# A second Strassen level for a third product: 82 matmul steps per output stage become 81

## The chip, the core and the metric

The kernel runs on one core of a Trainium2 chip. The metric is the device time of one execution in microseconds (us). Three runs of the kernel before took 2226.53, 2226.63 and 2226.74 us, a median of 2226.63 us.

## The reference

A convolution over the last seven positions of a sequence, with one softmax-normalised kernel per head, feeds a two-layer block with the hardswish activation. All of it is in float32.

```python
w = softmax(weight)                      # (8 heads, 7 taps)
x_pad = zeros(6 positions) ++ x          # x: (8, 4096, 192)
y[b, s, c] = sum_k w[head(c), k] * x_pad[b, s + k, c]
y = y.reshape(32768, 192)
h = y @ w_in                             # (192 -> 2048)
g = h * clip(h + 3, 0, 6) / 6
out = g @ w_out                          # (2048 -> 192)
```

## The kernel before

**Blocks.** The 32768 tokens are worked through in 32 blocks of 1024 (`NB`). Block 0 is handled by code of its own, in which the weights are prepared too. Each of the other 31 blocks runs `first_layer` and then `second_layer`. While block i is in its second layer, the convolution result `y` of block i+1 is split into three float32 parts (`split_high`, `split_rest`), which are swapped between the partition halves by DMA into `y_other` (`swap_parts`, six DMAs of 384 KB), and the input of block i+2 is loaded (`begin_conv`). The convolution steps (L919, L921) are placed among the other work.

**First layer.** 16 units (`count`) each compute 128 of the 2048 hidden channels for one pairing of token halves, 18 matmuls per unit. ScalarE (ACT) rescales the sum in PSUM and takes the relu, VectorE (DVE) multiplies (`gate`, L306) and writes into the tile `g`. A unit occupies one of four slots of two PSUM banks. Units 0 to 7 use `y_own`, units 8 to 15 `y_other`.

**Second layer as a Strassen product.** `g` is a 2 x 2 block matrix: rows are token halves of 512, columns halves of the hidden channels, 8 chunks of 128 each, named A11, A12, A21, A22. `w_out` is split in the same way. The Winograd form takes seven products instead of eight:

```
S1 = A21 + A22    S2 = S1 - A11    S3 = A11 - A21    S4 = A12 - S2
P1 = A11 B11   P2 = A12 B21   P3 = S4 B22   P4 = A22 T4
P5 = S1 T1     P6 = S2 T2     P7 = S3 T3
```

The sums are stored in place: S1 over A21, S2 over A11, and both S3 and S4 in the tile `s3`. So S1 needs S3 to have been formed, S2 needs P1 to be done with A11, and S4 needs P7 to be done with S3. S3 is formed pair of chunks by pair of chunks at the end of the first layer (three pairs on GpSimd, POOL, the last one on DVE). S1 is formed for two pairs by an adding DMA from POOL's queue (L557) and for the other two on DVE (L559). S2 and S4 are formed on DVE (`g_sums`, L412), four chunks at a time.

**Four streams.** A product has 96 output columns, in three quarters of 32. TensorE's array is used as four strips of 32 columns; `second_layer` writes one list of matmuls per strip (`streams`, `clock`), and sorts all of it by time. One step is half a matmul of 512 tokens, or one matmul of 256. Streams 0 to 2 take one quarter each of the plain products (`plain`, 8 matmuls of two steps per quarter). Stream 3 takes P1 and P5, whose first two quarters are computed with a second Strassen level (`small`): seven products of 4 matmuls of 256 tokens, over sums made by `small_sums` (L578) and weights made by `small_weights`. Their third quarter is plain. All streams have 82 steps:

```
streams 0, 1, 2:  P4  P7 (with one chunk of P1's third quarter)  P2  P6  P3
stream 3:         P1 (second level)  P5 (second level)
```

A finished accumulator is carried on by ACT copies: from one small accumulator to the next (`steps`), or from strip to strip, since a strip of the array writes only its own 32 partitions. `do(t, ...)` puts work of the other engines at step t of the program's order. Each engine works through its own part of that order and waits where an operand isn't ready; PE does so too, so a late operand in one stream stops all four.

**Tiles and banks.** Three of the four PSUM slots hold the accumulators d, e, b, x_, a and c; the fourth is free for the next first layer, except in the last block, where P3 is computed by token halves in it (`plain_by_halves`, `end_lower`, `end_upper`). The small accumulators A, B, C, E and V lie in the fourth strip's rows of banks that the other streams use too. `y_other` lies in a pool of its own (tag "other"), `p1` beside `s3`.

Of the kernel before, what the change touches and what calls it, by code (L numbers as in the profile page):

```python
# [25 lines left out]
def kernel(  # L26
# [93 lines left out]
    w_s = cst.tile([P, 2, 4, NP // 2, QS], F32, name="w_s")  # L120
# [144 lines left out]
    def swap(to, part):  # L265
        nc.sync.dma_start(out=to[D2:P], in_=part[0:D2])
        nc.sync.dma_start(out=to[0:D2], in_=part[D2:P])
# [222 lines left out]
    def swap_parts():  # L490
        y_other[0] = pools[0].tile([P, 3, K3, N], F32, name="y_other", tag="other")
        for n in range(3):
            swap(y_other[0][:, n], y_own[n])


    def first_layer(i, jobs):
# [92 lines left out]
    def second_layer(i, between):  # L589
        last = i + 1 == NB  # L590
        ours = [free_slots.pop(0) for _ in range(3)]
        d, e, b, x_, a, c = (psum[:, 2 * n + k] for n in ours for k in range(2))
        ends = [psum[:, 2 * free_slots[0] + k] for k in range(2)] if last else [b, b]
# [35 lines left out]
        def small(n, m_, out, start=False):  # L629

            x, w = prod[n]
            sums, ws = (s1[-1], w_s[:, 0]) if n == 1 else (s5, w_s[:, 1])
            x11, x12, x21, x22 = four_parts(x)
            z1, z2, z3, z4 = four_parts(sums)
            b11, b12, b21, b22 = (
                w_out[:, h::2, w, q * QS : (q + 1) * QS] for h in range(2) for q in range(2)
            )
            t1, t2, t3, t4 = (ws[:, k] for k in range(4))
            xm, wm = {
                1: (x11, b11), 2: (x12, b21), 3: (z4, b22), 4: (x22, t4),  # L640
                5: (z1, t1), 6: (z2, t2), 7: (z3, t3),
            }[m_]
            for u in range(NP // 2):
                put(3, 1, lambda u=u: matmul(
                    3, out[:, lo], wm[:, u], xm[:, u], start and u == 0
                ))
# [9 lines left out]
        def tiles():  # L656
            new_results()
            if last:
                xts.insert(0, NP - 1)
            late.update(zip(("p7", "p5", "u3"), (results[0][m, n] for n in range(3))))  # L660

        for q in range(NQ):
            plain(q, d, 4, q, every, True)
            before = (1, 6, NP)[q]
            plain(q, c, 7, q, every[:before], True)
            plain(q, e, 1, 2, range(5 + q, 6 + q))
            do(clock[q], copy, out=e[rows(q + 1)] if q < 2 else p1[third], in_=e[rows(q)])
            plain(q, c, 7, q, every[before:])
            plain(q, a, 2, q, every[:6], True)
            plain(q, b, 6, q, every)  # L670
            plain(q, a, 2, q, every[6:])
            if last:
                plain_by_halves(q, 3, q, 0)
                plain_by_halves(q, 3, q, 1)
            else:
                plain(q, b, 3, q, every)

        def level_two(n, p, chunks, order):
# [3 lines left out]
            def fill_half(t, k):  # L682
                for _ in range(k):
                    ch = left[t].pop(0)
                    x, w = prod[n]
                    put(3, 1, lambda ch=ch: matmul(
                        3, (ends[0], x_)[t][fourth, halves[t]], w_out[:, ch, w, 2 * QS : 3 * QS],
                        x[:, ch, halves[t]], ch == 0,
                    ))

            def fill(k):
# [3 lines left out]
                1: lambda: copy(out=B[:, lo], in_=A[:, lo]),  # L695
                2: lambda: copy(out=p()[first, lo], in_=A[:, lo]),
                6: lambda: copy(out=C[:, lo], in_=B[:, lo]),
                5: lambda: copy(out=p()[second, lo], in_=E[:, lo]),
                7: lambda: add(p()[second, hi], C[:, lo], p()[second, lo]),
                3: lambda: add(p()[second, lo], B[:, lo], p()[second, lo]),  # L700
                4: lambda: copy(out=p()[first, hi], in_=C[:, lo]),
            }
            to = {1: A, 2: A, 6: B, 5: E, 7: C, 3: B, 4: C}
            for step in order.split():
# [4 lines left out]
                else:  # L709
                    k = int(step)  # L710
                    small(n, k, to[k], k in (1, 5))
                    do(clock[3], steps[k])

        level_two(1, lambda: p1, range(5), "1 x5 6 5 2 7 3 4")
        do(14, copy, out=e[first], in_=V)
# [7 lines left out]
        for t, n in ((16.2, 1), (16.2, 2), (30.5, 3), (34.5, 4)):  # L723
            do(t, small_sums, s5, S1, (n,), nc.vector)
        do(32, tiles)
        do(34, lambda: copy(out=late["p7"], in_=c[m]))
# [3 lines left out]
        do(62, lambda: add(late["u3"], b[m], late["p7"]))  # L730
# [3 lines left out]
        do(66, lambda: store(i, p1, 0, 0))  # L734
# [9 lines left out]
        def end_lower():  # L744
            p5, u3, c12 = late["p5"], late["u3"], results[0][m, 6]
            two = slice(0, 2 * QS)
            copy(out=p5[third, lo], in_=ends[0][fourth, lo])
# [10 lines left out]
        def end_upper():  # L758
            p5, u3, c12 = late["p5"], late["u3"], results[0][m, 6]
            copy(out=p5[third, hi], in_=x_[fourth, hi])  # L760
# [4 lines left out]
            add(c12[third, hi], x_[fourth, hi], c12[third, hi])  # L765
# [3 lines left out]
        if last:  # L769
            do(74, end_lower)  # L770
        else:
            do(82, lambda: copy(out=late["p5"][third], in_=V))
# [28 lines left out]
    with tc.manual_schedule():  # L801
# [125 lines left out]
        def split_y():  # L927
            high, low, mix = y_own
            high_of(high[:], y[:])
            split_rest()  # L930
# [4 lines left out]
        def split_rest():  # L935
            high, low, mix = y_own
            nc.vector.tensor_tensor(out=r32(low[:]), in0=y[:], in1=high[:], op=ALU.subtract)
            from_high(mix[:], high[:], 1.0 + EPS, y[:], ALU.subtract)
# [29 lines left out]
        p1 = last.tile([DH, N], F32, name="p1")  # L968
        left = []
        for i in range(1, NB):  # L970
# [10 lines left out]
            if i + 1 < NB:  # L981
                between = [(13, split_high), (15, split_rest), (18, swap_parts)]
# [36 lines left out]
```

## Time and profile before

| | us |
|---|---|
| median of three runs | 2226.63 |
| profiled execution, span from first to last instruction | 2224.9 |
| median of the runs less that span | 1.7 |
| first layer, start to start (988.70 to 1021.60) | 32.90 |
| second layer (953.23 to 988.70) | 35.47 |
| POOL: one small sum L578, 128x256, in a row of its kind | 0.74 |
| POOL: one subtraction L412, 128x1024, mean | 3.07 |
| ACT: copy 32x256, PSUM to PSUM / to SBUF | 0.34 / 0.37 |
| ACT: copy 32x512, PSUM to PSUM / to SBUF | 0.55 / 0.58 |

A line of a group reads: line of the kernel, engine, operation, output<-inputs, shapes, count | busy us, mean ns of one | idle time before, and what ended it. A line of a stage has the stretch from the span's start, its length, then each engine's busy time with its number of instructions, the granted clock, the DMA engines' mean busy share and GB/s. PEld is TensorE's weight load, which overlaps its matmuls. A float32 matmul appears as two instructions in the profile. A line of the timeline has start, duration, engine, line and operation.

### The profile page before, as it was taken

The numbers are of one execution on the slowest core, as the hardware profiler recorded it, in microseconds if no ns is written. First come the engines' busy times: TensorE is split into PE (matmuls) and PEld (weight loads), VectorE is DVE, ScalarE is ACT, GpSimd is POOL, SyncE is SP. The second block draws the span as 40 slices with busy tenths as digits, with TensorE's granted clock in tenths as the row PEclk, the third lists the DMA queues.
The fourth block names the chain that finished last, engine by engine and source line by source line (L and its number), as shares of the span: only waits on it lengthen the run. The fifth ranks groups of instructions, "written<-read, shape, count | busy, mean of one in ns | idle before, by whom it ended". The sixth has DMA issues, their size and how long they took to land.

```text
span 2224.9 us, 50339 instructions
## 1 busy us (share of the span) xinstructions
PE 2218.0 (100%) x21496; PEld 1532.7 (69%) x21496; DVE 1894.3 (85%) x1673; ACT 1379.2 (62%) x1678; POOL 823.8 (37%) x690
## 2 busy tenths in 40 slices
PE   9999999999999999999999999999999999999999
PEld 5467776677766777766777667776677776677766
DVE  8888888888888888888888888888888888888876
ACT  7457665576655676555766557665567655576654
POOL 2344432344422444223443234442244422344323
PEclk9999999999999999999999999999999999999999
DMA  6244224443244342344422444324434234442232
GB/s 157 57 98 85 49 58 91 85 83 62 53 82 91 77 80 47 71 91 84 85 48 58 91 87 81 67 49 82 91 79 81 47 67 91 84 84 52 55 77 34
DMA packets 253584, 166.57 MB, mean 75 GB/s; under 512 B 208017, under 2 KB 213137, under 8 KB 253361
## 3 DMA queue, kind: packets, MB, share of 16 engines
q1 hardware_dynamic: 234872, 129.46, 28.4%
q0 software_dynamic: 17248, 33.64, 8.7%
q8 instruction: 168, 2.75, 0.5%
q14 instruction: 56, 0.45, 0.1%
q10 hardware_dynamic: 1240, 0.27, 0.1%
HBM read 31.72 MB, written 25.17 MB: 26 GB/s over the span
## 4 chain that ended last, share of the span: by engine, by line
PE 99%; DVE 0%; DMA 0%; ACTq 0%; issue 0%; DVEq 0%; ACT 0%
PE psum L615 49%; PE psum L508 46%; PE psum L296 2%; PE psum L341 2%; DMA x<-in_x_dram 0%; DVE y L255 0%; DVE top L175 0%; ACTq L89 0%; PE psum L816 0%; DVE results L456 0%; DVE scale L171 0%; DVE y L251 0%; DVE scale L192 0%; DVEq L1014 0%; DVE results L462 0%
## 5 line engine op out<-in xcount | busy, mean ns | idle before, releaser
L615 PE MATMUL psum<-g,w_out 128*32 128x512 f32 (+1 forms) x6712 | 967.5, 552 | 0.0
L306 DVE SCALAR_TENSOR_TENSOR g<-g,psum 128x1024 f32<-128x1024 f32 (+1 forms) x528 | 618.3, 1186 | 198.8 <-ACT g L302 194.5
L578 POOL TENSOR_TENSOR s<-g 128x256 f32<-128x256 f32 x248 | 273.6, 1103 | 1241.1 <-DVE g L306 1200.5
L302 ACT ACTIVATE g<-psum,half 128x1024 f32<-128x1024 f32 (+1 forms) x528 | 564.8, 1087 | 6.0 <-PE psum L508 5.2
L615 PEld LDWEIGHTS psum<-g,w_out 128*32 128x32 f32 x6712 | 371.8, 110 | 246.0 <-issue 126.7
L508 PE MATMUL psum<-y,w_in 64*128 64x512 f32 x4464 | 521.4, 388 | 0.0
L508 PE MATMUL psum<-y_other,w_in 64*128 64x512 f32 x4464 | 516.0, 386 | 0.0
L520 ACT ACTIVATE psum<-psum 128x1024 f32<-128x1024 f32 x465 | 469.0, 1008 | 50.7 <-PE psum L508 48.4
L508 PEld LDWEIGHTS psum<-y,w_in 64*128 64x128 f32 x4464 | 413.5, 184 | 115.7 <-issue 26.0
L508 PEld LDWEIGHTS psum<-y_other,w_in 64*128 64x128 f32 x4464 | 418.1, 184 | 87.8
L615 PE MATMUL psum<-s,w_out 128*32 128x512 f32 (+1 forms) x3272 | 465.5, 570 | 0.0
L921 DVE SCALAR_TENSOR_TENSOR y<-x,c_sb,y 128x1536 f32<-128x1536 f32 x186 | 335.2, 1802 | 2.6 <-ACT y L919 1.3
L412 POOL TENSOR_TENSOR s<-g 128x1024 f32<-128x1024 f32 x93 | 285.9, 3074 | 26.2 <-DVE g L306 26.2
L615 PE MATMUL psum<-g,w_s 128*32 128x256 f32 x1240 | 282.8, 379 | 0.0
L615 PEld LDWEIGHTS psum<-s,w_out 128*32 128x32 f32 x3272 | 154.3, 110 | 81.9 <-issue 49.4
L615 PEld LDWEIGHTS psum<-g,w_s 128*32 128x32 f32 x1240 | 136.4, 110 | 67.7
L412 DVE TENSOR_TENSOR s<-g 128x2048 f32<-128x2048 f32 (+1 forms) x93 | 181.3, 1977 | 1.1
L615 PE MATMUL psum<-s,w_s 128*32 128x256 f32 x744 | 170.7, 379 | 0.0
L578 DVE TENSOR_TENSOR g<-g 128x1024 f32<-128x1024 f32 x124 | 151.7, 1224 | 5.3
L412 DVE TENSOR_TENSOR g<-g 128x2048 f32<-128x2048 f32 x62 | 139.1, 2284 | 0.0
L612 ACT COPY psum<-psum 32x512 f32<-32x512 f32 x93 | 51.3, 551 | 135.4 <-PE psum L615 135.4
L456 DVE TENSOR_TENSOR results<-psum,results 32x256 f32<-32x256 f32 (+3 forms) x128 | 69.3, 541 | 50.9 <-issue 45.5
(91 smaller groups left out, 1299.5 us busy)
## 6 DMA issues: line engine op xcount, KB each, us to landing
y_other<-y SPq DMA_DIRECT2D x186, 384.0 KB, 5.1
g<-g POOLq DMA_DIRECT2D x62, 512.0 KB, 5.0
out_dram<-results SPq DMA_DIRECT2D x378, 64.0 KB, 2.0
x<-in_x_dram SPq DMA_DIRECT2D x53, 388.5 KB, 7.7
stage<-in_moe_w_in_dram SPq DMA_DIRECT2D x16, 192.0 KB, 4.5
stage<-in_moe_w_out_dram SPq DMA_DIRECT2D x8, 384.0 KB, 6.8
x<-in_x_dram SPq DMA_DIRECT2D x7, 384.0 KB, 8.4
x<-in_x_dram POOLq DMA_DIRECT2D x2, 388.5 KB, 5.4
```

The lines of the kernel that those rows point to most:

```text
L296: nc.tensor.matmul(out=psum[:, b], lhsT=w[r], rhs=src, start=start, stop=stop, skip_group_check=onto,)
L302: nc.scalar.activation(r6, h, ACT.Relu, bias=half[:], scale=1.0 / 6.0)
L306: nc.vector.scalar_tensor_tensor(out=g_, in0=g_, scalar=1.0, in1=h, op0=ALU.min, op1=ALU.mult)
L341: lambda p=p: nc.tensor.matmul(out=bank[j * QS : (j + 1) * QS, tokens], lhsT=w_out[:, p, w, cols], rhs=x[:, p, tokens], start=(first and p ...
L412: engine.tensor_tensor(out=o[:, r], in0=a[:, r], in1=b[:, r], op=op)
L456: nc.vector.tensor_tensor(out=out, in0=x, in1=y, op=op)
L508: nc.tensor.matmul(out=psum[:, 2 * slots[n] + k], lhsT=r32(w_in_parts[part][r, c, s]), rhs=r32(y_other[0][r, part, s] if group else y_own[ ...
L520: nc.scalar.mul(both(n), both(n), 4097.0)
L578: engine.tensor_tensor(out=o, in0=p, in1=q, op=op)
L612: streams[3].append((t - 0.5, lambda: fn(*args, **kw)))
L615: nc.tensor.matmul(out=out, lhsT=w, rhs=x, start=start, stop=True, tile_position=(0, j * QS), skip_group_check=True,)
L921: jobs.append(lambda k=k: nc.vector.scalar_tensor_tensor(out=y[:], in0=x[:, :, k : k + N], scalar=c_sb[:, k : k + 1], in1=y[:], op0=ALU.mu ...
```

## The change

- **P2** gets the second level too, in streams 0 and 1: its small products write accumulators A2, E2, B2, C2 in the fourth PSUM slot (banks f, h), over small sums `sums2` that DVE forms of A12 at the start of the stage, with a third set of small weights (of B21). Its third quarter is spread over all four streams (`by_half` takes one chunk for half the tokens), and its accumulator handed from strip to strip by ACT.
- **The streams** are dealt out anew, 81 steps each. P1 comes first in stream 3, with two of the eight chunks of its third quarter, while stream 2 does the other six.
- **Small accumulators** of P1 and P5 move into the fourth rows of the banks e and x_ alone, and their folding is two additions in one place (`fold`).
- **S1** is formed by adding DMAs in all four pairs; S3's third pair moves from POOL to DVE.
- **S4** is formed by ACT, which writes -S2 into `s3`, and an adding DMA that adds A12, in four pairs (`negative`).
- **z2**, a tile with `sums2` and `p1`, shares the buffer of `y_other`. So the six swaps into `y_other` come at step 70 instead of 18, and are issued by POOL instead of SyncE (SP). The split of `y` is taken apart: high part at step 9, low part at 20, mixed part at 46 (before: 13, 15, 15).

```diff
@@ first_layer
-                g_sums(nc.gpsimd if n + 1 < count else nc.vector, (3,), range(NP)[pair], 2)
-                if n + 3 < count:
-                    nc.gpsimd.dma_start(out=S1[:, pair], in_=A22[:, pair], accum_op=ALU.add)
-        for pair in (slice(NP - 2, NP), slice(NP - 4, NP - 2)):
-            add(S1[:, pair], A21[:, pair], A22[:, pair])
+                g_sums(nc.gpsimd if n + 3 < count else nc.vector, (3,), range(NP)[pair], 2)
+                nc.gpsimd.dma_start(out=S1[:, pair], in_=A22[:, pair], accum_op=ALU.add)
@@ second_layer
-        B, C, V = (bank[rows(3)] for bank in (x_, d, b))
-        A, E = e[rows(3)], a[rows(3)]
+        f, h = (psum[:, 2 * free_slots[0] + k] for k in range(2))
+        V = b[fourth]
+        A, E, B, C = (bank[fourth, t] for bank in (e, x_) for t in halves)
+        A2, E2, C2, B2 = f[first, lo], f[second, hi], h[first, lo], h[second, hi]
+        z = pools[0].tile([P, NP + 1, N], F32, name="z2", tag="other")
+        sums2, p1 = z[:, 0:NP], z[0:DH, NP]
+        def fold(p, m136):
+            add(p[second, hi], p[second, hi], p[second, lo])
+            add(p[second, lo], m136, p[second, lo])
+        def negative(pair):
+            nc.scalar.mul(S3[:, pair], S2[:, pair], -1.0)
+            nc.gpsimd.dma_start(out=S3[:, pair], in_=A12[:, pair], accum_op=ALU.add)
-        for q in range(NQ):
-            plain(q, d, 4, q, every, True)
...
-            plain(q, a, 2, q, every[6:])
+        plain(0, d, 4, 0, every, True)
+        small(2, 1, A2, True, 0)
+        after(0, copy, out=B2, in_=A2)
+        plain(0, c, 7, 0, every[:3], True)
+        by_half(0, a, 2, 2, 2, 1)
+        after(0, copy, out=a[fourth], in_=a[first])
+        plain(0, c, 7, 0, every[3:])
+        small(2, 7, C2, False, 0)
+        after(0, lambda: copy(out=p2(second, hi), in_=C2))
+        small(2, 2, A2, False, 0)
+        after(0, lambda: copy(out=p2(first, lo), in_=A2))
+        plain(0, b, 6, 0, every)
+        small(2, 4, C2, False, 0)
+        p3(0)
...
+        plain(1, a, 2, 2, every[:2], True)
+        by_half(1, a, 2, 2, 2, 0)
...
+        small(2, 6, B2, False, 1)
...
+        small(2, 5, E2, True, 1)
...
+        small(2, 3, B2, False, 1)
...
+        plain(2, b, 1, 2, every[2:])
+        after(2, copy, out=p1[third], in_=b[third])
...
-        level_two(1, lambda: p1, range(5), "1 x5 6 5 2 7 3 4")
+        level_two(1, lambda: p1, (), "1")
+        plain(3, b, 1, 2, every[:2], True)
+        after(3, copy, out=b[third], in_=V)
+        level_two(1, lambda: p1, (), "6 2 7 5 4 3")
+        plain(3, a, 2, 2, every[3:5])
+        by_half(3, a, 2, 2, 5, 0)
+        after(3, copy, out=a[third], in_=a[fourth])
-            "1 l4 2 6 5 7 3 l2 4 l2 h8" if last else "1 x2 2 6 5 7 3 x1 4 x5",
+            "1 l8 6 2 7 5 4 3 h8" if last else "1 x6 6 2 7 5 4 3 x2",
-        for t, n in ((16.2, 1), (16.2, 2), (30.5, 3), (34.5, 4)):
-            do(t, small_sums, s5, S1, (n,), nc.vector)
-        do(38, copy, out=b[m], in_=p1[:])
-        do(38, g_sums, nc.vector, (2,), every, 4)
-        do(38, g_sums, nc.vector, (4,), every, 4)
+        do(0, small_sums, sums2, A12, (1, 2, 3, 4), nc.vector)
+        do(28.5, g_sums, nc.vector, (2,), every[:4], 4)
+        do(33, g_sums, nc.vector, (2,), every[4:], 4)
+        do(35, copy, out=b[m], in_=p1)
+        do(45, small_sums, s5, S1, (1, 2, 3, 4), nc.vector)
+        for n, t in zip(range(0, NP, 2), (34, 39, 42, 45)):
+            do(t, negative, slice(n, n + 2))
-        do(66, add, p1[:], a[m], p1[:])
+        do(65.4, lambda: copy(out=p2(third, slice(0, N)), in_=a[third]))
+        do(65.4, lambda: copy(out=p2(first, hi), in_=C2))
+        do(65.4, lambda: fold(late["p2"], B2))
+        do(65.6, lambda: add(late["p2"], late["p2"], p1))
@@ begin_block_two
-            for n, w in enumerate((B11, T1)):
+            for n, w in enumerate((B11, T1, B21)):
                 small_weights(w_s[:, n], w)
@@ the loop over blocks
-                between = [(13, split_high), (15, split_rest), (18, swap_parts)]
+                between = [(9, split_high), (20, split_low), (46, split_mix), (70, lambda: swap_parts(nc.gpsimd))]
```

More of the change, by code (lines that the diff above doesn't have):

```diff
@@ L627, in plain, with by_half, small @@
                 ))
-        def small(n, m_, out, start=False):
+        def by_half(j, bank, n, q, ch, t, start=False):
             x, w = prod[n]
-            sums, ws = (s1[-1], w_s[:, 0]) if n == 1 else (s5, w_s[:, 1])
+            put(j, 1, lambda: matmul(
+                j, bank[rows(j), halves[t]], w_out[:, ch, w, q * QS : (q + 1) * QS],
+                x[:, ch, halves[t]], start,
+            ))
+        def small(n, m_, out, start=False, j=3):
+            x, w = prod[n]
+            sums, ws = {
+                1: (s1[-1], w_s[:, 0]), 5: (s5, w_s[:, 1]), 2: (sums2, w_s[:, 2]),
+            }[n]
             x11, x12, x21, x22 = four_parts(x)
@@ L660, in tiles, with after, p2, p3 @@
             late.update(zip(("p7", "p5", "u3"), (results[0][m, n] for n in range(3))))
-        for q in range(NQ):
-            plain(q, d, 4, q, every, True)
[L664 to L670, printed above, removed]
-            plain(q, a, 2, q, every[6:])
+            late["p2"] = results[0][m, 6]
+        def fold(p, m136):
[4 more added lines that the diff above has]
+            nc.gpsimd.dma_start(out=S3[:, pair], in_=A12[:, pair], accum_op=ALU.add)
+        def after(j, fn, *args, **kw):
+            do(clock[j], fn, *args, **kw)
+        def p2(r, t):
+            return late["p2"][r, t]
+        def p3(q):
             if last:
@@ L746, in end_lower @@
             two = slice(0, 2 * QS)
-            copy(out=p5[third, lo], in_=ends[0][fourth, lo])
+            copy(out=p5[third, lo], in_=a[fourth, lo])
             copy(out=c12[third, hi], in_=b[third, hi])
@@ L759, in end_upper @@
             p5, u3, c12 = late["p5"], late["u3"], results[0][m, 6]
-            copy(out=p5[third, hi], in_=x_[fourth, hi])
+            copy(out=p5[third, hi], in_=c[fourth, hi])
             add(c12[:, hi], ends[1][m, hi], c12[:, hi])
```

72 lines of the change are left out of this document (44 added, 28 removed).

## The prediction

> **What bounds the kernel now.** I read the summary page first: which engine is full, whether its clock is granted, and who is on the chain that ended last.
>
> ```profile
> PE 2218.0 (100%) x21496; PEld 1532.7 (69%) x21496; DVE 1894.3 (85%) x1673; ACT 1379.2 (62%) x1678; POOL 823.8 (37%) x690
> ...
> PEclk9999999999999999999999999999999999999999
> ...
> q0 software_dynamic: 17248, 33.64, 8.7%
> ...
> PE 99%; DVE 0%; DMA 0%; ACTq 0%; issue 0%; DVEq 0%; ACT 0%
> ...
> g<-g POOLq DMA_DIRECT2D x62, 512.0 KB, 5.0
> ```
>
> PE is busy all the time at full clock and makes up 99% of the chain: nothing else delays the end. So the time is the number of PE steps times their spacing, and a change gains if it takes steps away without making PE wait. Second, the busy time by stage, for one period in the middle (second layer, first layer, next second layer):
>
> ```profile
> core 0: us, PE busy (x) PEld busy (x) DVE busy (x) ACT busy (x) POOL busy (x), PEclk, DMA share, GB/s
> 953.23:988.70 35.47, 35.47 (x387) 21.15 (x385) 32.79 (x27) 11.89 (x20) 3.65 (x2) 1.00 0.59 120
> 988.70:1021.60 32.90, 32.90 (x289) 26.82 (x288) 25.86 (x23) 30.75 (x32) 21.68 (x19) 1.00 0.15 25
> ```
>
> A second layer takes 35.47 us, in which DVE is busy 32.79, ACT 11.89 and POOL 3.65. Its four PE streams have 82 steps each, so a step is 35.47 / 82 = 0.433 us. Third, the groups inside that stage give the durations:
>
> ```profile
> L578 DVE TENSOR_TENSOR g<-g 128x1024 f32<-128x1024 f32 x4 | 4.9, 1223 | 0.2
> L412 DVE TENSOR_TENSOR g<-g 128x2048 f32<-128x2048 f32 x2 | 4.5, 2284 | 0.0
> L412 DVE TENSOR_TENSOR s<-g 128x2048 f32<-128x2048 f32 x2 | 4.5, 2284 | 0.0
> ...
> L456 DVE TENSOR_TENSOR g<-g 128x1024 f32<-128x1024 f32 x2 | 2.4, 1221 | 0.0
> ...
> L412 DVE TENSOR_TENSOR s<-g 128x1024 f32<-128x1024 f32 x1 | 1.3, 1333 | 0.0
> ...
> L456 DVE TENSOR_TENSOR p<-psum,p 32x256 f32<-32x256 f32 x2 | 0.9, 427 | 0.3 <-PE psum L615 0.3
> ```
>
> Last, POOL beside DVE near the start, because the change gives POOL's queue more to do:
>
> ```profile
> 93.05 0.45 POOL L587 TENSOR_TENSOR w_s<-w_out 128x128 f32<-128x128 f32 x1
> ...
> 97.23 1.97 POOL L587 TENSOR_TENSOR w_s<-w_out 128x128 f32<-128x128 f32 x1
> ```
>
> The same operation takes 0.45 us beside a DVE transpose and 1.97 us beside DVE's convolution steps, which read two SBUF operands. Those two steps took 3.94 us together there; their mean is 1.80 each.
>
> **The change on PE.** Counted in steps, a plain product is 3 quarters x 8 chunks x 2 = 48, one with the second level 7 x 4 + 16 = 44. Before: 5 x 48 + 2 x 44 = 328 = 4 x 82. After: 4 x 48 + 3 x 44 = 324 = 4 x 81. The four streams as written add up to 81 each. One step less in each of 31 second layers: 31 x 0.433 = **-13.4 us**. There are 206 matmuls per stage instead of 192, because narrow ones (256 tokens) replace wide ones. Stream 3 already has 56 narrow ones of its 69 and keeps the pace of the rest, so I charge nothing for the 14.
>
> The rest has to stay hidden. I walk one stage; times with a plus count from its start.
>
> **DVE.** Per stage it loses S4's two subtractions (2 x 2.284) and S1's two additions (2 x 1.221), 7.0 us. It gains P2's four small sums (4 x 1.223), one S3 subtraction taken over from POOL (1.333) and P2's two folding additions (2 x 0.43), 7.1 us. The load is equal, so only the order can hurt. The row of the gates puts the third-last gate's end at +1.2. Then: S3 pair +2.5, two gates +4.9, S3 pair +6.3, P2's small sums +7.5, +8.7, +9.9, +11.2, the low part of y (1.75) +12.9, S2's first half +15.2, P1's two folds +16.1, S2's second half +18.4, P5's four small sums (they overwrite A22, which P4 reads until step 44, +19.0) +23.9, the mixed part of y +25.7. Needs: P2's second small sum at step 25 (+10.8, ready +8.7); S2 at steps 45 and 53 (+19.5 and +22.9, ready +15.2 and +18.4); P5's second small sum at step 53 (+22.9, ready +21.4); P6 read out of its bank (0.69) between its end at step 61 (+26.4) and P3's first write at step 65 (+28.1), done at +27.3. The smallest margins are 0.8 and 1.5 us. The read has the same four steps as before.
>
> **ACT.** It gains four negations. No row has one (SBUF to SBUF, 128x1024); nearest are 1.01 us (L520, from PSUM) and 1.48 for 1536 elements (L474, two thirds is 0.99), so 1.0 each. About eight copies of 32x256 (0.34 to 0.37) and two of 32x512 (0.55 to 0.58) come on top: 4.0 + 2.9 + 1.1 = 8.0 us, 11.9 to 19.9 of 35. Each copy between small accumulators has at least four steps (1.7 us) until its next matmul. The densest case, three copies around steps 20 and 21, ends near +10.1 against a need at step 26 (+11.3).
>
> **S4's chain** is new and crosses four queues: S2 on DVE, negation on ACT, issue on POOL, adding DMA, then P3 on PE. The first negation ends near +16.2; the second waits behind two copies (+18.3), the third and fourth behind S2's second half and four copies (+20.8, +22.2). An adding DMA of 512 KB lands 5.0 us after its issue, and 8.7% of the span over 62 of them is 3.1 us of all 16 engines each. So they land near +21.3, +24.4, +27.5, +30.6; P3 needs its pairs of chunks at steps 65, 69, 73, 77: +28.1, +29.9, +31.6, +33.3. Margins 6.8 down to 2.7 us: cost nothing. Bounds: 0, and what the first rival gives. In the last block P3 goes by token halves and needs its last pair at step 71 (+30.7); there the split of y is missing on DVE and ACT, which brings the chain some 1.5 us forward. I take 0, with 1 us as the bound.
>
> **S1** by DMA: the last pair is subtracted at +6.3, lands near +11.5, and is read at step 37 (+16.0).
>
> **POOL's queue** gets 4 adding DMAs, 2 more for S1 (1.20 us to issue) and the 6 swaps (0.65, the row of the two loads of x at 88 us), 11 us, and loses one 2.5 us subtraction; it was idle from about +4 to +44. The swaps wait for DVE's last reading of p1 (about +30) and land by about +45, if 2.4 MB take the 12 us that six swaps and a load of x take now. The first layer needs them half way, near +51. SP's queue loses them, so x is loaded earlier, under the first layer, where the DMA share is 0.15. Four more small-weight operations near the start (0.45 to 1.97 each) lie before POOL's first small sums, which the second layer at 133 us is the first to need.
>
> Does DVE hold up POOL's issuing? Treated like the small-weight rows, the first S4 issue would wait for S2's second half, from +16.3 to +18.4, and the last landing would be +32.7, still before +33.3. The Trainium skill (SBUF — State Buffer, Who interferes with whom) says that a DVE instruction with two SBUF inputs contends with POOL instructions that read SBUF and not with those that only write. The small-weight rows agree with the first half; no run here shows the second half for a DMA's issue, and by it the landing stays at +30.6. The sum is the same either way.
>
> **Sum.** The profiled execution has a span of 2224.9 us; the median of the runs is 2226.63, so 1.7 us lie around it. 2224.9 - 13.4 = 2211.5, and 2213.2 as a median.
>
> **Rivals.**
> 1. *S4 comes too late* (slower). If one adding DMA takes its full 5.0 us before the next begins, they land at +21.3, +26.3, +31.3, +36.3: the last is 3.0 us late, 31 x 3.0 - 13.4 = +80, 2306 us. It decides against the change from 0.43 us late per stage, at 4.1 us per DMA. For it: the change triples such DMAs, and 6 x 31 x 3.1 us raise the DMA share by 26 points. Against: 3.1 is measured, and after x and the swaps have left the stage little else runs then.
> 2. *DVE's chain slips* (about no change). Where POOL worked beside them, the two convolution steps each took 0.17 longer. Some 11 two-operand operations lie between +6.3 and +25.7: 1.9 us, so P6 is read 1.2 us later than +27.3, P3 waits 0.4, and 31 x 0.4 = 12 takes the gain back: about 2226. Against: POOL computes nothing in that time any more, it only issues.
> 3. *Streams out of phase* (slower). Single narrow matmuls shift streams 1, 0, 3 and 2 by half a wide matmul, at steps 20 to 44; before, narrow ones come in fours. If each shift costs a step: 31 x 4 x 0.433 - 13.4 = +40, 2267. Against: narrow and wide streams already run side by side at 0.433 per step. The Trainium skill (TensorE: Matmul & The Clock Gate, Measured speedup vs the span model) says matmuls start and end in program order. The trace disagrees: stream 3's narrow ones come behind the wide ones in the program and end before them, or the 56 would not fit into 35.47 us.
>
> **Chances and range.** Forecast 0.73, rival 1 0.14, rival 2 0.08, rival 3 0.05. A measurement of this kernel can tell 0.2% (4.5 us) from no change. Faster: the forecast and a weak form of rival 2, 0.74; same 0.06; slower 0.20. Around the forecast alone 2210 to 2217 (0.1 us per stage either way, and the last block); up to rival 2 and a small lateness of S4, 2210 to 2230.
>
> **What the changed profile would show.** Second layers of 35.0 us and first layers of 32.9; no PE wait on a DMA at P3; DVE's busy time within 10 us of 1894; ACT near 1630; q0 near three times its share plus the swaps. Wrong, if PE's releasers name the DMA into S3 (rival 1) or DVE (2), or if stages are longer with no releaser (3).

## The result, and the profile after

The changed kernel takes 2216.98 us (median of 5 runs, 2215.85 to 2218.15) against 2226.63 before: a ratio of 0.9956, 95% interval 0.9944 to 0.9969. The forecast was 2213.2. The direction and the mechanism were right, and 3.8 us of the 13.4 us gain were lost on the way. The new runs spread over 2.3 us, where the old ones spread over 0.2.

The page of the changed kernel: busy times, the busiest DMA queue, shares of the chain of waits, then groups (after the bar: total us, mean ns | idle time before it and what ended it) and DMA issues (median us to landing).

```profile
PE 2208.0 (100%) x22364; PEld 1581.8 (71%) x22364; DVE 1900.8 (86%) x1766; ACT 1615.0 (73%) x2112; POOL 1021.9 (46%) x1029
...
q0 software_dynamic: 82240, 201.95, 48.5%
...
PE 98%; ACT 1%; DVE 0%; DMA 0%; issue 0%; DVEq 0%; ACTq 0%
...
L575 POOL TENSOR_TENSOR s<-g 128x256 f32<-128x256 f32 x248 | 228.9, 923 | 426.7 <-DMA out_dram<-results 422.6
L986 DVE SCALAR_TENSOR_TENSOR y<-x,c_sb,y 128x1536 f32<-128x1536 f32 x186 | 346.0, 1860 | 2.6 <-ACT y L984 1.3
...
y_other<-y POOLq DMA_DIRECT2D x180, 384.0 KB, 8.8
g<-g POOLq DMA_DIRECT2D x124, 512.0 KB, 5.9
...
out_dram<-results SPq DMA_DIRECT2D x378, 64.0 KB, 4.3
```

PE is still the bound, at 98% of the chain and at full clock throughout. Three rows differ from before in a way that the forecast did not have. POOL's small sums for P1 (L575, `s<-g`) now wait 422.6 us in all for stores of results. Those stores land 4.3 us after their issue, where before they took:

```profile
out_dram<-results SPq DMA_DIRECT2D x378, 64.0 KB, 2.0
```

And the convolution steps on DVE (L986, which was L921) have a mean of 1860 ns, where it was 1802:

```profile
L921 DVE SCALAR_TENSOR_TENSOR y<-x,c_sb,y 128x1536 f32<-128x1536 f32 x186 | 335.2, 1802 | 2.6 <-ACT y L919 1.3
```

One second layer and the first layer behind it, as busy time by stage (start and end; then length, and busy us of each engine with its instruction count; clock, DMA share, GB/s):

```profile
core 0: us, PE busy (x) PEld busy (x) DVE busy (x) ACT busy (x) POOL busy (x), PEclk, DMA share, GB/s
200.72:235.77 35.05, 35.05 (x415) 22.75 (x414) 32.22 (x29) 19.57 (x34) 13.43 (x14) 1.00 0.83 142
235.77:268.98 33.21, 33.20 (x289) 26.75 (x288) 27.21 (x26) 30.75 (x32) 20.39 (x19) 1.00 0.48 105
```

The second layer is 0.42 us shorter than the 35.47 before, and PE has no gap in it. The first layer is 0.31 us longer than the 32.90 before, with PE, by its row, hardly idle either: its row is modelled from the ends of matmuls, so short waits hide in it. Adding up such stages for the whole span gives the account (profiled executions, 2217.5 us and a span of 2215.7 for the new one):

| part | before, us | after, us | difference |
|---|---|---|---|
| start, up to the first of the 31 first layers | 99.81 | 99.84 | +0.03 |
| 31 first layers | 1020.09 (each 32.90 to 32.94) | 1023.12 (32.90 to 33.27) | **+3.03** |
| 30 second layers | 1064.18 (35.47 each, one 35.58) | 1051.28 (each 35.04) | **-12.90** |
| last second layer | 35.58 | 35.45 | -0.13 |
| PE's end to the end of the span | 5.26 | 6.04 | +0.78 |
| sum | 2224.93 | 2215.73 | -9.2 |

35.04 is 81 x 0.4326: the step was saved in full, in every stage. What was lost lies in the first layers, which the diff does not touch. The chain of waits named PE there, not the cause; what ended the small waits is in the row of waits, in which PE's weight loads for the first layer wait for a free PSUM slot, that is for the gate (L306) on DVE. Columns: total us, times, longest. Before (the row by itself), POOL's sums waited for DVE's gate, whose result they read.

```profile
POOL s L575 <- DMA out_dram<-results: 422.6, 30, 14.5
...
PEld psum L508 <- DVE g L306: 4.9, 16, 0.5
```

```profile
POOL s L578 <- DVE g L306: 1200.5, 63, 40.4
```

The timeline shows why a gate is late. In the first layer from 235.77, DVE from +23.5 on (start, duration):

```profile
259.29 1.22 DVE L306 SCALAR_TENSOR_TENSOR g<-g,psum 128x1024 f32<-128x1024 f32 x1 [0.82 <-ACT g L302]
260.43 2.38 DVE L986 SCALAR_TENSOR_TENSOR y<-x,c_sb,y 128x1536 f32<-128x1536 f32 x1
```

and POOL in the same stretch:

```profile
259.76 0.74 POOL L575 TENSOR_TENSOR s<-g 128x256 f32<-128x256 f32 x1
260.46 0.74 POOL L575 TENSOR_TENSOR s<-g,s 128x256 f32<-128x256 f32 x1
261.15 3.92 POOL L412 TENSOR_TENSOR s<-g 128x1024 f32<-128x1024 f32 x1
```

The convolution step began, at 260.43, while POOL was at its small sums (an operation from 259.76 to 260.50, the next right behind it), and took 2.38 us instead of the 1.81 of an undisturbed one. The POOL operation after those, L412 from 261.15, in turn takes 3.92 us, where the 62 of its kind have a mean of 2.69. The gate behind the convolution step came late, and the next PE unit waited for its slot. The longest of the sixteen waits is 0.5 us.

From these rows came the first theory, a chain of five links. **(a)** The swaps come from POOL's queue at step 70 and land between +35 and +46 (medians of the six), at the same time as the block's stores. **(b)** Beside them the stores land late, at up to 13.7 us. **(c)** The tile `s1` shares the buffer of `results`, from which the stores read, so P1's small sums start at +13.5 of the first layer instead of +8.55. **(d)** There POOL has a backlog, is at work when convolution steps begin, and prolongs them (37 take over 1.9 us). **(e)** The gates behind those are late and PE waits for slots. The rival was that the loss is not POOL's but belongs to the DMA traffic or the new DVE order, with the late sums only beside it.

### The profile page after: what moved, and what is told of

It is laid out like the page before. It is cut to its first block, busy times and chain, and to the rows that moved or that the text cites. A ratio compares the mean times of both kernels' runs of the same rounds, so it can differ in the third digit from the quotient of the medians.

```text
span 2215.7 us, 53039 instructions
## 1 busy us (share of the span) xinstructions
PE 2208.0 (100%) x22364; PEld 1581.8 (71%) x22364; DVE 1900.8 (86%) x1766; ACT 1615.0 (73%) x2112; POOL 1021.9 (46%) x1029
## 3 DMA queue, kind: packets, MB, share of 16 engines
q0 software_dynamic: 82240, 201.95, 48.5%
q1 hardware_dynamic: 220472, 58.67, 14.7%
## 4 chain that ended last, share of the span: by engine, by line
PE 98%; ACT 1%; DVE 0%; DMA 0%; issue 0%; DVEq 0%; ACTq 0%
PE psum L616 48%; PE psum L508 45%; PE psum L296 2%; PE psum L341 2%; DMA s<-g 0%; PE psum L881 0%; ACT g L302 0%; PE psum L889 0%; ACT psum L520 0%; ACT s L678 0%; DVE g L306 0%; DVE y L986 0%; DVE results L456 0%; DVE results L462 0%; ACT results L791 0%
## 5 line engine op out<-in xcount | busy, mean ns | idle before, releaser
L616 PE MATMUL psum<-g,w_out 128*32 128x512 f32 (+1 forms) x6340 | 899.5, 525 | 0.0
L306 DVE SCALAR_TENSOR_TENSOR g<-g,psum 128x1024 f32<-128x1024 f32 (+1 forms) x528 | 616.5, 1183 | 181.8 <-ACT g L302 181.4
L616 PE MATMUL psum<-s,w_out 128*32 128x512 f32 (+1 forms) x3272 | 503.7, 570 | 0.1
L575 POOL TENSOR_TENSOR s<-g 128x256 f32<-128x256 f32 x248 | 228.9, 923 | 426.7 <-DMA out_dram<-results 422.6
L986 DVE SCALAR_TENSOR_TENSOR y<-x,c_sb,y 128x1536 f32<-128x1536 f32 x186 | 346.0, 1860 | 2.6 <-ACT y L984 1.3
L679 POOL DMA_DIRECT2D s<-g x124 | 148.5, 1202 | 335.5 <-ACT s L678 293.0
L616 PEld LDWEIGHTS psum<-s,w_out 128*32 128x32 f32 x3272 | 176.4, 110 | 60.1 <-issue 33.0
L556 POOL DMA_DIRECT2D g<-g x124 | 150.0, 1214 | 106.5 <-issue 63.7
L616 PEld LDWEIGHTS psum<-g,w_s 128*32 128x32 f32 x1488 | 159.2, 110 | 42.6
L613 ACT COPY psum<-psum 32x512 f32<-32x512 f32 x186 | 89.4, 481 | 112.7 <-PE psum L616 109.3
L616 PE MATMUL psum<-z,w_s 128*32 128x256 f32 x744 | 170.6, 379 | 0.0
L412 POOL TENSOR_TENSOR s<-g 128x1024 f32<-128x1024 f32 x62 | 166.8, 2691 | 0.8 <-DVE g L306 0.8
L575 DVE TENSOR_TENSOR g<-g 128x1024 f32<-128x1024 f32 x124 | 146.3, 1221 | 11.7 <-PE psum L616 8.5
```

The source lines that it names most:

```text
L306: nc.vector.scalar_tensor_tensor(out=g_, in0=g_, scalar=1.0, in1=h, op0=ALU.min, op1=ALU.mult)
L412: engine.tensor_tensor(out=o[:, r], in0=a[:, r], in1=b[:, r], op=op)
L575: engine.tensor_tensor(out=o, in0=p, in1=q, op=op)
L613: streams[3].append((t - 0.5, lambda: fn(*args, **kw)))
L616: nc.tensor.matmul(out=out, lhsT=w, rhs=x, start=start, stop=True, tile_position=(0, j * QS), skip_group_check=True,)
L679: nc.gpsimd.dma_start(out=S3[:, pair], in_=A12[:, pair], accum_op=ALU.add)
```

## The experiments

Two chips were used, the first for the first four runs and the second for the last four. The kernel before takes 2227.78 on the one (15 runs) and 2227.98 on the other (9 runs), and most first layers without a wait take 32.95 on both instead of 32.90. So ratios and stages are compared, not times across chips. "The changed kernel" with no other mark is the profile above.

### Two stores from another buffer

```diff
-        xt = next_xt()
+        xt = next_xt() if xt is None else xt
...
-            store(i, u3 if k else p5, k, 1)
+            store(i, u3 if k else p5, k, 1, xt=A12[:, NP - 1 - k])
```

> The changed kernel, but the last two transposed results of a block (the ones stored at the start of the next first layer) go into rows of A12 that are free then, so the first-layer small sums on POOL need not wait for these stores to land. Theory 1 (stores held up by the swaps delay POOL's small sums, these then run beside DVE's convolution steps and prolong them, and a late gate makes PE wait): small sums start near +8.5 us of the first layer instead of +12 to +14, all first layers are 32.9 us long, the 3.0 us lost there come back: about 2214, and runs agree within 0.5 us. Theory 2 (DVE's own work at the turn of the stages is late, POOL has no part in it): first layers stay as in the changed kernel, up to 33.3 us, about 2217.

Measured: 2217.08 us (2216.81 to 2217.66, 5 runs), ratio 0.9952 (0.994 to 0.9965). The small sums start at a median of +10.9; twelve convolution steps are still over 1.9 us, all at +16.5; the first layers sum to 1022.86, 1.4 us above 31 x 32.95. What held POOL now is spread over five rows of its waits, of which these are the largest (the other two have 23.7 and 10.8 us):

```profile
POOL s L575 <- DMA out_dram<-results: 122.9, 11, 11.4
POOL s L575 <- DMA out_dram<-g: 105.0, 9, 11.9
POOL s L575 <- DVE g L306: 86.4, 19, 12.0
```

Half of an answer. The sums moved forward by half the way, and part of the prolonged steps went with them, but the block's two other stores (p7's and p2's) still use the buffer. The time is the 2217 of theory 2, but on a chip where the kernel before takes 1.15 us more than in the result; the 1.4 us in the first layers lie between the two theories. It takes all four stores to tell, which is the run `e6_all_xt` below.

### POOL writes instead of reading

```diff
-                small_sums(s1[-1], A11, (1, 2, 3, 4), nc.gpsimd, every[n - 1 : n + 1])
+                for part in four_parts(s1[-1][:, n - 1 : n + 1]):
+                    nc.gpsimd.memset(part, 0.0)
```

> The changed kernel, but POOL's small sums of P1 are replaced by as many memsets of the same shape (the first two quarters of P1 are wrong by that); POOL still waits for the stores, but reads nothing while DVE runs the convolution. Theory 1: no convolution step is longer than 1.9 us beside them (now up to 2.4) and the PE waits of 0.3 to 0.4 us in the second half of the first layers go where the small sums were the partner; waits that go with POOL's 128x1024 subtraction may stay. Total 2214 to 2215. Theory 2: the waits stay, 2217.

Measured: 2215.71 us (one run). All first layers are 32.90 to 32.95 long, and PE waits for no gate in them. POOL still started at +13.6, and the stores were as late as in the changed kernel:

```profile
L987 DVE SCALAR_TENSOR_TENSOR y<-x,c_sb,y 128x1536 f32<-128x1536 f32 x186 | 335.4, 1803 | 2.6 <-ACT y L985 1.4
...
out_dram<-results SPq DMA_DIRECT2D x378, 64.0 KB, 4.3
```

So with the late stores and the swaps in place, DVE's steps have their old mean as soon as POOL does not read SBUF. That is link (d), and it excludes the DMA traffic by itself as a cause. The memsets are also shorter (0.31 us each against 0.74 in the timeline above), so that POOL has less of a backlog. But 30 of the convolution steps that the timeline lists singly begin while a memset is running, and each takes 1.81 or 1.82 us. The Trainium skill (SBUF — State Buffer, Who interferes with whom) says that a DVE instruction with two SBUF inputs contends with a POOL instruction that reads SBUF and not with one that only writes it. Those 30 steps show the second half of the rule, which nothing in the trace of before did.

### The old kernel with late swaps from POOL

```diff
-                between = [(13, split_high), (15, split_rest), (18, swap_parts)]
+                between = [(13, split_high), (15, split_rest), (70, lambda: swap_parts(nc.gpsimd))]
```

> The kernel before, with nothing changed but the six swaps: at step 70 instead of 18, issued by POOL instead of SP. Theory 1: the stores land later (median 4 us instead of 2.0), POOL's small sums start 3 to 5 us later than at +8.9, and some first layers are 0.1 to 0.4 us longer: 2227 to 2231, with runs 1 to 2 us apart. Theory 2: first layers unchanged, 2226.6.

Measured: 2228.35 us (10 runs) against 2227.78, ratio 1.0003 (0.9993 to 1.0012). The time lies in the 2227 to 2231 of theory 1 only because this chip is slower. The late stores and late sums that theory 1 expected did not come (2.0 us, and +8.57), and the profile says why:

```profile
y_other<-y POOLq DMA_DIRECT2D x180, 384.0 KB, 5.2
out_dram<-results SPq DMA_DIRECT2D x378, 64.0 KB, 2.0
```

The swaps did not come late at all: they were issued at +4 to +11 of the stage and had landed by +18. In that kernel `y_other` has a buffer of its own and POOL has nothing else to do by then, so step 70 of the written order is reached at once. A place in the order is not a time. The run still separates two things: POOL's queue as such costs little (0.57 us between the medians), and what makes the swaps late in the changed kernel is that z2 shares `y_other`'s buffer, so that they wait for p1's last reader. In the changed kernel's stage from 200.72, DVE's addition that reads p1 ends at +30.8 and the first swap is issued at +31.3; in the run with S4 back on DVE (below, the stage from 777.66) that addition ends at +33.6, and the median of the first issues is +34.2.

### The changed kernel with the swaps behind the stores

```diff
-                between = [(9, split_high), (20, split_low), (46, split_mix), (70, lambda: swap_parts(nc.gpsimd))]
+                between = [(9, split_high), (20, split_low), (46, split_mix)]
...
-            jobs[-1] = left + conv[3:4]
+            jobs[-1] = left + ([swap_parts] if i > 1 else []) + conv[3:4]
```

> The changed kernel, but the six swaps are issued by SP behind the last six stores of a block, in the next first layer. Theory 1: the stores land in about 2 us again, small sums start near +8.5 and the waits on a gate go; in their place PE may wait for the swapped parts, needed at +15.6, +16.4 and +19: by twelve microseconds for all six they land near +18, a margin of 1 us or nothing. 2214 if they come in time, 2220 or more if not. Theory 2: waits on a gate as in the changed kernel, 2217 or more.

Measured: 2217.45 us (one run). SP issues the swaps behind the block's last stores, and links (b) to (e) are gone together: the stores land in 2.0 us, the small sums start at +8.57 and wait for what they read, and no convolution step is prolonged. In their place PE waits, in some blocks, for the swapped parts:

```profile
POOL s L575 <- DVE g L306: 607.8, 63, 20.0
...
PEld psum L508 <- DMA y_other<-y: 1.6, 4, 0.6
...
out_dram<-results SPq DMA_DIRECT2D x378, 64.0 KB, 2.0
```

First layers reach 33.62, and their sum of 1023.55 is still 2.1 us above 31 x 32.95. The time lies between the 2214 and the 2220 that were expected. So it was indeed the swaps that delayed the stores, (a) to (b), but moving them behind the stores makes them too late themselves.

### The changed kernel again, and all four stores from another buffer

The first is the changed kernel on the second chip, beside the second:

```diff
-        do(62, lambda: store(i, late["p7"], 1, 0))
+        do(62, lambda: store(i, late["p7"], 1, 0, xt=None if last else A11[:, NP - 1]))
...
-        do(65.6, lambda: store(i, late["p2"], 0, 0))
+        do(65.6, lambda: store(i, late["p2"], 0, 0, xt=None if last else A11[:, NP - 2]))
...
-            store(i, u3 if k else p5, k, 1)
+            store(i, u3 if k else p5, k, 1, xt=A12[:, NP - 1 - k])
```

> The changed kernel, nothing altered, to stand beside the next ones on one chip. Second layers 35.04 us, first layers between 32.9 and 33.3, 3 us above their minimum in sum; ratio 0.9945 to 0.9965.

> The changed kernel, but the transposed results of all four stores of a block go into rows of A11 and A12 that are free then (the last block excepted), so POOL's small sums wait for no store at all. Theory 1 (late stores, late small sums, a prolonged convolution step, a late gate): small sums start at +8.5 in every block, no convolution step over 1.9 us, all first layers within 0.05 us of their minimum, 3 us less than the changed kernel beside it: ratio 0.9935 to 0.9945. Rival (the small sums are held by something else, or the second layer's own DMA traffic disturbs them): start stays at +11 and the first layers keep 1.5 to 3 us.

Measured: 2218.57 us (2217.24 to 2219.48, 5 runs) for the changed kernel, ratio 0.9957 (0.9945 to 0.997); 2215.62 us (2215.24 to 2216.04, 5 runs) with the four stores moved, ratio 0.9944 (0.9931 to 0.9958). The first in groups and waits:

```profile
L986 DVE SCALAR_TENSOR_TENSOR y<-x,c_sb,y 128x1536 f32<-128x1536 f32 x186 | 347.3, 1867 | 2.6 <-ACT y L984 1.4
...
POOL s L575 <- DMA out_dram<-results: 393.2, 28, 14.5
...
PEld psum L508 <- DVE g L306: 6.1, 19, 0.5
```

The second:

```profile
L986 DVE SCALAR_TENSOR_TENSOR y<-x,c_sb,y 128x1536 f32<-128x1536 f32 x186 | 335.4, 1803 | 2.6 <-ACT y L984 1.3
...
POOL s L575 <- DVE g L306: 302.6, 64, 9.2
...
out_dram<-g SPq DMA_DIRECT2D x360, 64.0 KB, 4.3
```

Here the swaps and the stores are as late as in the changed kernel (4.3 us), and only link (c) is cut: POOL no longer waits for a store and starts at +8.57. The steps are back at 1803, the wait for a slot is gone from PE's waits, and the first layers sum to 1021.42 (31 x 32.95 = 1021.45) against 1025.31 beside it. The 2.95 us between the medians are the loss that was to be found (in the two profiled executions the first layers differ by 3.9, and the start and the last second layer give back 0.8 of it), and the spread of the runs falls from 2.2 to 0.8 us. This version beats both kernels.

In one point the theory was wrong. It had only late sums run beside DVE's convolution steps, so that in this kernel they would no longer meet. They do meet. The timeline of POOL in its first layer from 236 on, at the first and the ninth of its sums:

```profile
244.47 2.24 POOL L575 TENSOR_TENSOR s<-g 128x256 f32<-128x256 f32 x1 [9.13 <-DVE g L306]
246.79 0.73 POOL L575 TENSOR_TENSOR s<-s,g 128x256 f32<-128x256 f32 x1
...
252.62 2.25 POOL L575 TENSOR_TENSOR s<-g 128x256 f32<-128x256 f32 x1 [0.79 <-DVE g L306]
```

and of DVE:

```profile
244.30 1.81 DVE L986 SCALAR_TENSOR_TENSOR y<-x,c_sb,y 128x1536 f32<-128x1536 f32 x1
...
252.46 1.81 DVE L986 SCALAR_TENSOR_TENSOR y<-x,c_sb,y 128x1536 f32<-128x1536 f32 x1
```

Both begin behind the same gate, and the convolution step is first, by 0.17 and 0.16 us. Then POOL's sum takes 2.25 us instead of 0.74, and DVE's step nothing more. In the changed kernel POOL comes with a backlog and is first, and DVE pays. Sorting the convolution steps that the timelines list singly by who was at work when they began:

| kernel | POOL reading already at work | POOL's read just behind it |
|---|---|---|
| before | none | 90, each 1.81 us |
| changed | 59, mean 1.99, up to 2.42 us | 3, each 1.81 us |
| changed, four stores moved | 1, 2.01 us | 90, 1.81 or 1.82 us |

So the late start does not create the collision but turns it round: it moves the wait from POOL, which has time to spare, to DVE, which has none. The Trainium skill says so in the same section (SBUF — State Buffer, Who interferes with whom): the order of issue decides which of the two blocks, and the second waits for the first. This trace agrees, with 2.25 against 0.74 on the one side and up to 2.42 against 1.81 on the other.

### The price of DVE without S4 by negation

The forecast had DVE's load unchanged because negation and the adding DMAs take S4 from it. This run gives S4 back to DVE as two subtractions:

```diff
-        for n, t in zip(range(0, NP, 2), (34, 39, 42, 45)):
-            do(t, negative, slice(n, n + 2))
+        do(45.5, g_sums, nc.vector, (4,), every, 4)
```

> The changed kernel, but S4 is formed by DVE in two subtractions of 128x2048 right behind P5's small sums, as in the kernel before, instead of by four negations and adding DMAs. By the prediction's walk along DVE the mixed part of y ends 4.6 us later, at +30.3, P6 is read out of its bank until +31.0 instead of +27.3, and P3's first write, due at +28.1, waits 2.9 us: second layers of 37.9 us in 30 blocks, 2217 + 87 = 2304. If DVE has more room than the walk says (or PE is held up by something else), second layers stay below 36.5, under 2260.

Measured: 2324.54 us (one run). PE waits for DVE to read P6 out of its bank, and two of its stages are 39.78 and 38.10 us long (columns as above):

```profile
PEld psum L616 <- DVE results L456: 67.0, 30, 2.7
```

```profile
346.69:386.47 39.78, 37.97 (x415) 21.99 (x413) 37.01 (x32) 15.79 (x30) 8.09 (x10) 0.96 0.45 80
777.66:815.76 38.10, 36.29 (x414) 21.42 (x413) 36.37 (x32) 15.79 (x30) 8.05 (x10) 1.00 0.42 72
```

The wait is at the place that the walk over DVE's order names, 2.2 us each (67.0 / 30); behind it come 1.0 us each for a copy by ACT (L751, 28.9 us in 29 waits). Of the 30 stages 22 have a median of 38.1 us, where 37.9 was expected. The other eight take 39.8 to 40.0: in them the granted clock falls, to 0.96 in the mean of the stage, which the walk does not have (more on it at the end). Without S4's new way the change would have made the kernel 97 us slower than before on that chip, instead of 9 faster.

### S4 later

```diff
-        for n, t in zip(range(0, NP, 2), (34, 39, 42, 45)):
+        for n, t in zip(range(0, NP, 2), (46, 51, 54, 57)):
```

> The changed kernel, but the four negations stand twelve steps later in the order (46, 51, 54, 57). This takes S4's margin away and measures rival 1's price. The changed kernel's adding DMAs landed at +21.6, +24.6, +27.7, +30.5; with the first negation ending near +20.8 they should land at +25.9, +29.0, +32.0, +35.1 against +28.1, +29.9, +31.6, +33.3: the last pair 1.8 us late, second layers of 36.9 us, 2217 + 56 = 2273. If P3 has slack that the steps do not show, second layers stay near 35.04 and the time near 2217.

Measured: 2475.9 us (one run), against 2273 expected. The four adding DMAs land at +27.0, +29.9, +32.8 and +36.9, the last 3.6 us late where 1.8 were expected, and the second layers average 39.1 us. But half of the loss lies elsewhere: the first layers sum to 1152.6, some 130 us more, one at 32.9 and another at 40.8 (columns as above):

```profile
482.20:522.96 40.76, 35.63 (x292) 31.12 (x288) 25.84 (x23) 30.85 (x32) 22.03 (x19) 0.92 0.42 88
561.68:594.58 32.90, 32.90 (x293) 26.83 (x289) 25.91 (x23) 30.76 (x32) 18.51 (x19) 1.00 0.48 100
```

The timeline of DVE, in the first layer from 482.20, has the reason:

```profile
491.55 0.71 DVE L462 STREAM_TRANSPOSE results<-results 96x512 f32<-96x512 f32 x1 [6.42 <-DMA out_dram<-results]
492.18 1.77 DVE L986 SCALAR_TENSOR_TENSOR y<-x,c_sb,y 128x1536 f32<-128x1536 f32 x1
493.88 1.21 DVE L306 SCALAR_TENSOR_TENSOR g<-g,psum 128x1024 f32<-128x1024 f32 x1
```

A transpose for a store waits 6.42 us for an earlier store that still reads the buffer it is to write. DVE's gate stands behind it, and PE waits 5.1 us for that gate. It is link (b) again, in a harsher form. The swaps are issued at +31.3 as before, but land at +39.9 to +48.4 instead of +35.1 to +45.6, behind the late adding DMAs. The stores beside them take 8.4 us in the median (18.2 at most), and the late stores hold a buffer. This reading rests on the trace alone; no run took the store's wait away here.

## Why the prediction was right or wrong

- **PE, 31 x 0.433.** Right to the hundredth: 35.04 us in each of 30 stages. Rival 3 is excluded, since fourteen more narrow matmuls and streams half a matmul out of phase cost nothing that the stage length shows. (The sentence of the Trainium skill that rival 3 draws on, in TensorE: Matmul & The Clock Gate, stands under The mechanism, one heading above the one named there.)
- **DVE's order, needs and margins.** Right: in no second layer does PE wait for DVE, and busy time is 1900.8 us, 6.5 more than before and within the 10 allowed. But 10.8 us of extra convolution time (346.0 against 335.2) are the very fault that was missed, and the order itself came out lighter. The run with S4 back on DVE shows that there was no room for it.
- **ACT and the queue of POOL's DMAs.** 1615.0 us busy; near 1630 was forecast. q0 has 48.5%, where three times its share and the swaps were forecast. The three was a slip: six adding DMAs on top of two per block make four times 8.7, 34.8; with the 13.7 that the swaps took from q1 (28.4% before, 14.7% now) that is the 48.5 measured.
- **S4's chain.** Landings forecast at +21.3, +24.4, +27.5 and +30.6; medians measured +21.6, +24.6, +27.7 and +30.5. The stacking by 3.1 us each, and not by 5.0 (rival 1), was right, although these DMAs take 6.6 us from issue in the median:

```profile
s<-g POOLq DMA_DIRECT2D x124, 512.0 KB, 6.6
```

In the last block the last pair landed at +30.9 against a need at +30.7, and PE lost 0.3 us (the stage takes 35.45, and 35.15 in the same kernel's other trace, where the pair landed at +30.2): 0 was taken and 1 was the bound.
- **S1 by DMA.** Its last pair landed at +13.3 in the median, not at +11.5; the need at +16.0 was met.
- **What rival 1 would have cost.** Its place was right and its price too small: the stage's lateness was counted, and not what follows in the first layer. It set 3.0 us of lateness at 31 x 3.0 = 93 us; the run with 3.6 us of it lost 257 against the changed kernel beside it (2475.9 and 2218.6).
- **POOL's queue: the step that failed.** It followed the swaps to their landing at about +45 (measured: medians up to +45.6), asked whether the first layer would need them sooner, and charged nothing. It did not ask what else moves at that time. The block's stores do, on SP's queue, and they landed in 4.3 us instead of 2.0; whoever waits for their buffer is late next, which is POOL's small sums, then DVE, then PE. Cost taken 0; measured 3.0 us in the profile, and 2.95 between two kernels that differ in that buffer alone.
- **Rival 2** had the right mechanism in the wrong place. It feared DVE's two-operand operations beside POOL's computing in the second layer, and dismissed it, rightly, because POOL only issues there. It happened in the first layer, to the convolution steps. The 0.17 us that it took from two steps near the start became 0.18 in the mean of 59 (1.99 against 1.81) and up to 0.61.
- **The end of the span.** 0.78 us of tail were not in the sum. In the last block P5 is folded at step 73, where it came around step 66, because its small products come in another order in that block. ACT's last copy before the end came 0.75 us after PE's end instead of 0.40. This is read from the two chains of waits, and not tested.

In the profiled execution the gain is 9.2 us where 13.4 was forecast. 3.0 (first layers), 0.8 (the end) and 0.3 (the last second layer gained 0.1 instead of 0.4) are 4.1 of the 4.2 missing. That execution took 2217.5, 0.5 above the median, which makes it, to 0.1, the 3.8 us by which the median misses the forecast.

The median lies just inside the 2210 to 2217 that the prediction gives around the forecast alone, and that is luck. The width stood for 0.1 us per second layer either way and for the last block; the second layers came out exact, and most of the miss lies in the first layers, for which it allowed nothing.

## What to carry to other kernels

When a transfer moves to another queue and time, look not only at whether its own reader gets it soon enough, but at every other transfer under way then, and follow that one's buffer to whoever reuses it. A loss can appear in a stage that the diff does not touch, three engines away from the edit, and the busy rows hide it: the row of waits and the stage lengths show it. Where two tiles share a buffer, the place at which an operation is written says little on when it runs; the last reader of the buffer does.

## What the hardware did that was not expected

- **A wait can cost PE more than its length.** In the run with S4 later, PE waited 5.1 us for the gate above. The granted clock in stretches around it:

```profile
core 0: us, PE busy (x), PEclk, DMA share, GB/s
488.00:490.00 2.00, 2.00 (x18) 1.00 1.04 230
490.00:494.00 4.00, 0.01 (x2) 0.94 0.71 106
494.00:498.00 4.00, 2.86 (x14) 0.50 0.30 47
498.00:502.00 4.00, 4.00 (x29) 0.70 0.00 0
502.00:512.00 10.00, 10.00 (x92) 1.00 0.01 2
```

The clock is at a half for some 6.9 us (0.5 + 4 + 2.4, by the three shares). The 43 matmuls in 2.86 + 4.00 us would have taken 43 x 0.109 = 4.7 us at the pace of the last line (10.00 / 92): 2.2 us lost on top of the 5.1. And in the run with S4 back on DVE, a wait of 1.72 us, in the stage from 346.69, was enough:

```profile
374.00:378.00 4.00, 2.19 (x25) 1.00 0.00 0
378.00:382.00 4.00, 4.00 (x30) 0.58 0.34 52
```

That is half the clock for some 3.4 us (4 x 0.42 / 0.5). Eight of that run's 30 stages have such a stretch and are 1.7 to 1.9 us longer than the rest, seven of them after a wait of 1.7 us. The other 22, with waits of 1.7 to 1.9 us, kept their full clock, the stage from 777.66 among them. So the length of the wait does not decide. Each of the eight slow stretches lasts 3.413 us in the trace's record of the clock, and they begin whole multiples of that apart (the first two, at 377.98 and 664.70, 84 of them). Counted from the points of that grid, the eight waits begin at 0.1 to 0.6 us, and the other 22 at 0.6 to 2.1. It matters where a wait falls in the grid; by which rule, stays open, since in the run with S4 later a wait of 1.8 us that began at 0.1 us kept the clock. The Trainium skill (TensorE: Matmul & The Clock Gate, Part 1) says that the array falls to half its clock after at least one idle window of about 3.4 us, and that the window runs freely. The grid agrees with the second half, and the wait of 5.1 us with the first. The waits of 1.72 us don't: they are half a window, and here the measurement decides. A sum that counts waits alone can be too low, here by 1.7 us in a stage (39.78 against 38.10), which is a part of why the last two runs came out above what was expected.

- **Small stores suffer beside large transfers.** 64 KB stores went from 2.0 to 4.3 us in the median, 13.7 at most, when swaps of 384 KB from POOL's queue ran beside them; with those moved away they were back at 2.0.
- **The same collision costs one engine or the other.** Starting 0.16 us behind DVE, POOL pays up to 1.5 us; starting ahead of it, DVE pays up to 0.6. Neither engine's busy time tells which without the order of their starts.
